# The order of 1230 tasks on five engines, replaced by another order

## The chip, the cores and the metric

The kernel runs on one core of a Trainium2 chip. The core has five engines with a queue each, which work their queues in order: TensorE (PE: matmuls into PSUM banks; PEld is its weight load), VectorE (DVE), ScalarE (ACT), GpSimd (POOL) and SyncE (SP, which here issues nearly all DMAs). Engines wait for each other by semaphores. The metric is the device time of one execution in microseconds (us).

## The reference, cut to what matters

One transformer block on 2048 tokens of width 512, all weights bfloat16. The modulation vectors come from a condition `c`; the attention is linear, with softmax features of 16 elements per head (32 heads), and a gated feed-forward part follows.

```python
mod = (_silu(c) @ w_mod).reshape(c.shape[0], 6, 1, -1)      # sa, ca, ga, sb, cb, gb
h = _layernorm(x) * (1 + ca) + sa
q, k, v = split_heads(h @ wqkv)
phi = lambda t: concat(softmax(t @ w_phi), softmax(-(t @ w_phi)))
kv, z = einsum(phi(k), v), sum(phi(k))                       # over all tokens
o = einsum(phi(q), kv) / (einsum(phi(q), z) + 1e-6)
x = x + ga * (o @ wo)
h = _layernorm(x) * (1 + cb) + sb
x = x + gb * ((sigmoid(h @ w_gate) * (h @ w_up)) @ w_down)
```

## The kernel before, in words

Tokens are cut into 16 tiles of 128. Everything is written as small tasks, each with its engine, what it reads and writes, and the buffers it uses. A string, `ORDER`, lists all 1230 tasks by name; `G.arrange` walks it, gives each task its engine (the default one, or the one behind an `@`: A is ACT, D is DVE, P is POOL), hands out buffer slots in that order, and the tasks are then emitted one by one. So the string alone sets what follows what in each engine's queue, and which earlier task must have let go of a buffer or of one of the eight PSUM banks.

```python
t.eng = LETTER[e] if e else next(iter(t.alts))
assert t.eng in t.alts and t.deps <= done and t not in done, name
for b in t.bufs:
    if b.slot is None:
        b.slot = slots[b.cls].pop(0)
```

The tasks by name, with their lines:
- `ld_...` are loads on SP (x in seven pieces, L537; the first two modulation blocks in four, L542; the key weights `wk`, L545, and value weights `wv`, L551; the attention gate's block `wmga`, L555; the rest of `w_mod`, `wmm2`, L556). `wqT0` to `wqT3` (L669) load the query weights by a DMA that transposes them.
- `warm...` (L600) are matmuls on zeros that nobody reads. `ld_wd2`, which writes the rows that they read, waits for all of them.
- `modc1.0` and `modc1.1` (L630) are the first modulation's products, in two halves of the width, 16 matmuls of one column each; `modc1c0`, `modc1c1` copy the sums.
- `tpw`, `wTc`, `fold1j`, `foldc1j` transpose the key weights on PE and multiply them by the feature weights (L661 to L685); `fold0j`, `foldc0j` do that for the query weights, `fold0j` reading what `wqTj` brought.
- `st1`, `rs1`, `nmr1`, `xn1` are the first layernorm; `tph` (L744) transposes a tile group on PE and `hm1` (L751, L753) modulates it. Layernorm groups are the tiles 0, 1, (2,3), (4,5) and so on; `hm1_23` is block 3 of group 2. Groups 6 and 7 are transposed by DMA (`xT1`, L736).
- `K`, `V`, `Q` (L817, L821, L871) are four matmuls of 512 columns for a tile, K in two halves for tiles 0 to 7 (`K0a` needs only blocks 0 and 1) and V for tiles 0 to 3. `e`, `n`, `r`, `phi` make the key features: exponentials on ACT (L776), sums on DVE (L780), reciprocals, products on DVE or POOL (L787); tiles 11 and 13 to 15 are cut in four or two parts. `qe`, `qn`, `qphi` and a DMA transpose `pT` do it for the queries. `va` copies V. `kv` (L282) adds up over tiles; `kvn`, `kvz` (L294, L299) read the sums out.
- Per tile then `num`, `rd`, `u` (attention out), `oT`, `out` (L356), `x1`, the second layernorm `st2` to `xn2`, `xnT`, `mod` (the second modulation), and per chunk of tiles (1, 1, 2, 4, 4, 4) the gated part: `g`, `u` (L447), `tg` (ACT), `hm` (DVE), `y` (L485), `fin`, and the store `st`.

`num0a` is the first task that needs the sum over all tokens; PE does `Q` of seven tiles ahead of it and of the others behind it.

Of the kernel before, what the change touches and what calls it, by code (L numbers as in the profile page):

```python
# [43 lines left out]
wqT1 hm1_22 hm1_13@A hm1_03 xn1_7 K1a K0a hm1_02@A hm1_23@A xn1_6 tph42 tph40 xn1_5 hm1_40@A st1_8 tph41 ld_x3a xn1_4 K3a hm1_42 hm1_12@A ld_wv0 nmr1_6 tph43
K3b hm1_41@A xn1_11 tph30 xn1_10 st1_9 rs1_5@P hm1_30@A tph31 wqT3 tph32 K1b ld_wmga st1_15 st1_14 hm1_31@A fold01 foldc01 K0b tph33 wqT2 rs1_8@P K2a K2b
hm1_33 nmr1_5 V0a wqT0 V0b V3a xn1_9 e3.0 V1a xT1_11 e0.0 fold03 n3.0 V1b nmr1_8 xn1_14 va0 e2.0 n0.0 st1_13 r0.0 modca.0 modca.1 xn1_15 st1_12 xn1_8 foldc03
n2.0 modcac e1.0 hm1_32@A V2a fold02 phi0.0 n1.0 r1.0 fold00 V2b foldc02 foldc00 r3.0 va1 xT1_10 hm1_60@P ld_wmm2 va2 r2.0@A hm1_62@P tph82 hm1_82@A tph50
phi2.0@D phi1.0@D hm1_50@A hm1_63@P V3b K4a K4b rs1_7@P Q0 Q2 kv0.0 Q1 qe0.0 va3 qe2.0 hm1_43@A qe1.0 modc2.0 tph52 modc2.1 tph51 nmr1_7 xn1_12 xn1_13
phi3.0@D ld_wo qn0.0 modc2c e4.0 kv1.0 qn2.0 hm1_52 kv2.0 Q4 K5a kv3.0 xT1_12 xT1_13 qphi0.0@P qphi0.1@P qn1.0 qe4.0 qphi2.1 tph80 K5b hm1_80@A hm1_51@A e5.0
pT0 qphi2.0 n4.0 r4.0@A qn4.0 n5.0 phi4.0@D qphi1.1@P hm1_61@P qphi1.0@P tph53 V5 K7a V4 va5 hm1_53@A V6 pT2 hm1_70@P qphi4.1 va4 hm1_71 mask4 va6 K6a K7b K6b  # L50
e6.0 K8 tph83 hm1_83 r5.0 qphi4.0@P e8.0 pT1 pT4 ld_wd2 tph81 hm1_81 n6.0 n8.0 e7.0 n7.0 V7 kv4.0 hm1_72@P K11 K9 V9 K14 V8 r6.0@A e9.0 va7 va9 r7.0@A e11.2
# [4 lines left out]
kv14.0 kv15.0 qn6.0 kvn0 kvz0 kv13.4 kv14.4 kv15.4 kvz1 kvn1 num0a num1a num2a wo2 rd0a wo_all rd1a qe3.0 u0a num0b num4a num1b rd0b Q11 qe5.0 rd2a u0b u2a
rd4a num2b qn3.0 u1a rd1b tpo0 Q8 qphi6.0@P qphi6.1@P oT0 out0 num4b rd2b u1b wd0 qe11.0 u2b qphi3.1@P qphi3.0@P x1_0 rd4b st2_0 qe8.0 Q7 qe7.0 tpo1 oT1 Q10
Q9 out1 Q15 oT2 rs2_0 qn5.0 nmr2_0 xn2_0 u4a u4b x1_1 qn7.0 tsw xnT0 out2 qphi5.1@P qphi5.0@P pT6 mod02 mod00 qphi7.0@P pT3 mod03@A mod01@A qe15.0 qphi7.1@P
Q13 g0.8 x1_2 tg0.8 g0.1 st2_1 wd1 rs2_1 tg0.1 u0.8 u0.1 g0.0 num3b g0.4 hm0.1 hm0.8 pT5 qe9.0 tg0.4 g0.9 wd2 u0.4 u0.9 rd3b u3b tg0.9 g0.5 num3a hm0.4 hm0.9
# [999 lines left out]
```

## Time and profile before

| what | us |
|---|---|
| three runs | 204.16, 204.36, 204.45 (median 204.36) |
| the profiled execution, first to last instruction (its span) | 202.6 |
| granted TensorE clock over the span | 1.000 |

The profiled execution's time is given by its span alone; its distance to the median of the runs is 1.8 us, which lies around the span. In the views below PE, PEld, DVE, ACT and POOL are the engines; "x16" is a count; in the timeline and the chain the first number is the start in us, the second the length; in brackets stands how long the engine sat idle before, and what ended that.

### The profile page before, as it was taken

How to read it: one execution, taken by the hardware profiler on the slowest of the kernel's cores; microseconds unless marked ns; L12 is line 12 of the kernel's file. 1: busy time of each engine (PE TensorE's matmuls, PEld its weight loads, DVE VectorE, ACT ScalarE, POOL GpSimd, SP SyncE). 2: the span in 40 equal slices, each digit the busy share in tenths (PEclk: the TensorE clock that was granted, in tenths of full speed). 3: DMA queues.
4: the chain of work that ended last, by engine and by line, in shares of the span. 5: the costliest groups of instructions: out<-in, count | busy, mean ns of one | idle time of the engine just before them, and what ended most of it. 6: DMA issues, size and time to landing. Idle time of an engine off the chain costs nothing.

```text
span 202.6 us, 4159 instructions
## 1 busy us (share of the span) xinstructions
PE 195.7 (97%) x1471; PEld 106.2 (52%) x1471; DVE 160.4 (79%) x375; ACT 106.1 (52%) x252; POOL 102.8 (51%) x144
## 2 busy tenths in 40 slices
PE   7889999999999999999999999999999999999993
PEld 2455565455464787668844444444444444444442
DVE  3899999999999999998897797884969754326622
ACT  3899999999978984566441215212113320334100
POOL 5598987888699998866670066230030332000000
PEclk9999999999999999999999999999999999999999
DMA  6999966559953962419645233542113031000011
GB/s 173 329 248 265 264 237 119 111 80 290 402 204 71 137 102 59 80 28 108 128 75 84 53 71 84 102 107 53 26 26 81 2 78 52 31 3 22 33 53 55
DMA packets 49452, 22.92 MB, mean 113 GB/s; under 512 B 38065, under 2 KB 47634, under 8 KB 49426
## 3 DMA queue, kind: packets, MB, share of 16 engines
q1 hardware_dynamic: 48896, 22.59, 48.9%
q8 instruction: 12, 0.20, 0.4%
q14 instruction: 14, 0.11, 0.2%
q10 hardware_dynamic: 530, 0.02, 0.1%
HBM read 11.58 MB, written 2.10 MB: 68 GB/s over the span
## 4 chain that ended last, share of the span: by engine, by line
PE 69%; DVE 14%; ACT 6%; issue 3%; POOL 3%; DMA 3%; SPq 1%; DVEq 0%; POOLq 0%
PE y_ps L485 19%; PE u_ps L447 18%; PE g_ps L447 17%; DVE ks L780 7%; PE a_ps L356 6%; DMA wqk_sb<-in_A_wqkv_dram 3%; PE num L326 2%; DVE kr L798 2%; ACT qe L776 2%; DVE phi L787 2%; PE q_ps L871 1%; PE g_ps L449 1%; ACT h1T L751 1%; DVE qks L780 1%; POOL phi L787 1%
## 5 line engine op out<-in xcount | busy, mean ns | idle before, releaser
L457 ACT ACTIVATE tg<-g_ps 128x512 bf16<-128x512 f32 (+5 forms) x66 | 28.8, 455 | 67.0 <-PE g_ps L447 39.4
L485 PE MATMUL y_ps<-wd_sb,wmod_sb 128*128 128x512 bf16 (+4 forms) x187 | 45.7, 367 | 0.0
L468 DVE SCALAR_TENSOR_TENSOR wmod_sb<-tg,u_ps 128x512 bf16<-128x512 bf16 (+4 forms) x63 | 30.2, 491 | 18.1 <-ACT tg L457 11.6
L447 PEld LDWEIGHTS <-wg_sb 128*128 128x128 bf16 (+1 forms) x252 | 21.9, 99 | 16.1
L447 PEld LDWEIGHTS <-wu_sb 128*128 128x128 bf16 (+1 forms) x252 | 21.9, 99 | 16.0 <-issue 0.3
L784 POOL TENSOR_TENSOR qphi<-qe,qks 128x512 bf16<-128x512 bf16 x24 | 25.1, 1062 | 4.4 <-DMA pT<-qphi 1.7
L485 PEld LDWEIGHTS <-wmod_sb 128*128 128x128 bf16 (+1 forms) x187 | 17.1, 98 | 16.0 <-issue 0.6
L447 PE MATMUL u_ps<-wT_sb,wu_sb 128*128 128x512 bf16 (+2 forms) x124 | 23.8, 322 | 0.0
L447 PE MATMUL g_ps<-wT_sb,wg_sb 128*128 128x512 bf16 (+2 forms) x124 | 23.2, 322 | 0.0
L447 PE MATMUL g_ps<-wqk_sb,wg_sb 128*128 128x128 bf16 (+4 forms) x128 | 20.0, 287 | 0.0
L447 PE MATMUL u_ps<-wqk_sb,wu_sb 128*128 128x128 bf16 (+4 forms) x128 | 19.8, 287 | 0.1
L780 DVE TENSOR_REDUCE qks<-qe 128x64 bf16<-128x1024 bf16 x16 | 19.2, 1206 | 0.0
L492 DVE TENSOR_TENSOR ot<-y_ps,x 128x512 bf16<-128x512 f32 (+2 forms) x17 | 11.1, 654 | 10.2 <-PE y_ps L485 10.1
L780 DVE TENSOR_REDUCE ks<-e 128x64 f32<-128x1024 bf16 (+2 forms) x22 | 19.1, 903 | 0.0
L376 POOL TENSOR_SCALAR ve<-mv 128x2 f32<-128x2 f32 (+1 forms) x8 | 1.8, 221 | 33.8 <-DVE mv L366 33.7
L776 ACT ACTIVATE e<-k_ps 128x512 bf16<-128x512 f32 (+2 forms) x44 | 18.2, 522 | 0.0
L776 ACT ACTIVATE qe<-q_ps 128x512 bf16<-128x512 f32 x32 | 17.4, 618 | 0.6 <-POOL phi L787 0.4
L817 PE MATMUL k_ps<-wqk_f,h1T 128*128 128x512 bf16 x64 | 16.5, 379 | 0.0
L356 PE MATMUL a_ps<-wo_sb,oT 128*128 128x512 bf16 x64 | 16.3, 379 | 0.0
L787 POOL TENSOR_TENSOR phi<-e,kr 128x1024 bf16<-128x1024 bf16 (+2 forms) x10 | 14.4, 1449 | 3.5 <-ACT kr L795 2.0
L821 PE MATMUL v_ps<-wv_sb,h1T 128*128 128x512 bf16 x64 | 16.1, 379 | 0.1
L871 PE MATMUL q_ps<-wqk_f,h1T 128*128 128x512 bf16 x64 | 15.9, 379 | 0.0
(132 smaller groups left out, 306.7 us busy)
## 6 DMA issues: line engine op xcount, KB each, us to landing
out_dram<-ot SPq DMA_DIRECT2D x15, 128.0 KB, 1.7
x_sb<-in_A_x_dram SPq DMA_DIRECT2D x6, 256.0 KB, 5.4
wmod_sb<-in_w_mod_dram SPq DMA_DIRECT2D x1, 1536.0 KB, 6.8
wu_sb<-in_B_w_up_dram SPq DMA_DIRECT2D x1, 1376.0 KB, 10.7
wg_sb<-in_B_w_gate_dram SPq DMA_DIRECT2D x1, 1376.0 KB, 10.6
wd_sb<-in_B_w_down_dram SPq DMA_DIRECT2D x1, 1280.0 KB, 7.7
wmod_sb<-in_w_mod_dram SPq DMA_DIRECT2D x4, 256.0 KB, 6.3
wqk_sb<-in_A_wqkv_dram SPq DMA_DIRECT2D x2, 256.0 KB, 4.8
```

The costliest lines, as they stand in the source:

```text
L356: pe.matmul(ap_[:], lhsT=oT[:, j, :], rhs=wo_sb[:, j, :], start=(j == 0), stop=(j == KT - 1))
L447: pe.matmul(ps[:fsz, 0:n], lhsT=w[:, j, ft * P:ft * P + fsz], rhs=h[:, j, 0:n], start=(j == 0), stop=(j == KT - 1))
L457: G.add(f"tg{k}.{ft}", {"ACT": 0.13 + n * 0.00083}, lambda e, tg=tg, g_ps=g_ps, fsz=fsz, n=n: act.activation(tg[:fsz, 0:n], g_ps[:fsz, 0:n ...
L468: dve.scalar_tensor_tensor(hm_all[:fsz, hm[k].slot, ft, 0:n], tg[:fsz, 0:n], 1.0, u_ps[:fsz, 0:n], op0=ALU.add, op1=ALU.mult)
L485: mm = pe.matmul(y[:, 0:c1 - c0], lhsT=hm_all[:fsz, hm[k].slot, ft, tl * P:(tl + 1) * P], rhs=wd_sb[:fsz, ft, c0:c1], start=(ft == 0), sto ...
L776: act.activation(ee[:, a:b, s].rearrange("p g f h -> p g (f h)"), kp[:, a * 64:b * 64].rearrange("p (g n) -> p g n", n=64), ACT.Exp, scale ...
L780: dve.tensor_reduce(ks[:, a:b].rearrange("p g s h -> p (g s) h"), ee[:, a:b].rearrange("p g s f h -> p (g s) h f"), axis=AX.X, op=ALU.add)
L784: engine(e).tensor_tensor(ph[:].rearrange("p (g s f h) -> p g s f h", s=2, f=DH, h=4)[:, :, s], ee[:, :, s], ks[:, :, 1 - s].unsqueeze(2). ...
L787: engine(e).tensor_tensor(ph[:, a * P:b * P].rearrange("p (g f h) -> p g f h", f=DH, h=4), ee[:, a:b].rearrange("p g s f h -> p (g s) f h" ...
L817: pe.matmul(kp[:], lhsT=h1T[:, j, t * P:(t + 1) * P], rhs=wqk_f[:, j, D:2 * D], start=(j == 0), stop=(j == KT - 1))
L821: pe.matmul(vp[:], lhsT=h1T[:, j, t * P:(t + 1) * P], rhs=wv_sb[:, j, :], start=(j == 0), stop=(j == KT - 1))
L871: pe.matmul(qp[:], lhsT=h1T[:, j, t * P:(t + 1) * P], rhs=wqk_f[:, j, 0:D], start=(j == 0), stop=(j == KT - 1))
```

## The change

The string `ORDER` is replaced by another; nothing else of the kernel changes (the new string has one line less, so lines behind it are numbered one lower). All tasks stay; their places change on all engines, and for some of them the engine. The first lines of the two:

```diff
-wdz pmem warm0 ld_x0a st1_1 rs1_1 st1_0 c1 c2 ld_x0b warm1_0 warm1_1 warm1_2 warm1_3 ld_wk0 ld_wk1 nmr1_1 xn1_1@A st1_3 warm1_4 st1_2 rs1_0 xn1_0 tph11 tpw1
...
+wdz pmem warm0 ld_x0a st1_0 c1 ld_x0b st1_2 warm1_0 warm1_1 st1_3 rs1_2 warm1_2 warm1_3 warm1_4 rs1_0@P xn1_0 warm1_5 warm1_6 warm1_7 ld_wk0 tpw0 wTc0 tpw1 wTc1
```

**SP's queue, the loads of the first 20 us.** `x_sb` is the input, `wmod_sb` the first modulation blocks, `wv_sb` the value weights, `wT_sb` the transposed query weights, and `wqk_sb<-in_w_mod_dram` the attention gate's block. Before:

```order
L542 DMA wmod_sb<-in_w_mod_dram 128x4x256 x2
L537 DMA x_sb<-in_A_x_dram 128x2x512
L542 DMA wmod_sb<-in_w_mod_dram 128x4x256 x2
L537 DMA x_sb<-in_A_x_dram 128x2x512
L669 DMA_TRANSPOSE wT_sb<-in_A_wqkv_dram 128x4x128
L537 DMA x_sb<-in_A_x_dram 128x4x512
L551 DMA wv_sb<-in_A_wqkv_dram 128x4x512
L669 DMA_TRANSPOSE wT_sb<-in_A_wqkv_dram 128x4x128
L555 DMA wqk_sb<-in_w_mod_dram 128x4x512
L669 DMA_TRANSPOSE wT_sb<-in_A_wqkv_dram 128x4x128 x2
```

The same place of the change:

```order
L541 DMA wmod_sb<-in_w_mod_dram 128x4x256 x2
L536 DMA x_sb<-in_A_x_dram 128x2x512
L541 DMA wmod_sb<-in_w_mod_dram 128x4x256 x2
L536 DMA x_sb<-in_A_x_dram 128x4x512
L536 DMA x_sb<-in_A_x_dram 128x2x512
L550 DMA wv_sb<-in_A_wqkv_dram 128x4x512
L668 DMA_TRANSPOSE wT_sb<-in_A_wqkv_dram 128x4x128
L554 DMA wqk_sb<-in_w_mod_dram 128x4x512
L668 DMA_TRANSPOSE wT_sb<-in_A_wqkv_dram 128x4x128 x3
L555 DMA wmod_sb<-in_w_mod_dram 128x4x1536
```

The transpose that stood ahead of the last x piece and the value weights now stands in the group of three behind the gate's block; the transposes come in the order 2, 0, 1, 3 (before 1, 3, 2, 0).

**PE's queue, around the second modulation half.** `tp_h` are the transposes of layernormed tiles, `k_ps` is a key product, `modc_ps` the modulation's sum, of which the first of 16 matmuls is shown. Before:

```order
L744 LDWEIGHTS xn
L744 MATMUL tp_h<-ident,xn 128x128
L744 LDWEIGHTS xn
L744 MATMUL tp_h<-ident,xn 128x128
L630 LDWEIGHTS wmod_sb
L630 MATMUL modc_ps<-sc_bf,wmod_sb 128x1
```

The change:

```order
L743 LDWEIGHTS xn
L743 MATMUL tp_h<-ident,xn 128x128
L816 LDWEIGHTS h1T
L816 MATMUL k_ps<-wqk_f,h1T 128x512
L816 LDWEIGHTS h1T
L816 MATMUL k_ps<-wqk_f,h1T 128x512
L743 LDWEIGHTS xn
L743 MATMUL tp_h<-ident,xn 128x128
L629 LDWEIGHTS wmod_sb
L629 MATMUL modc_ps<-sc_bf,wmod_sb 128x1
```

`K0a`, two matmuls, and a transpose now stand ahead of `modc1.1`; before, the first key product came behind it.

**ACT's queue, around the folded query weights.** `e<-k_ps` are the exponentials of key tiles, `vaug<-v_ps` copies of V, `wqk_f<-fold_ps` the copies `foldc0j`. Before:

```order
L685 CAST wqk_f<-fold_ps 128x512
L776 ACTIVATE e<-k_ps 128x8x64 x4
L836 CAST vaug_110<-v_ps 128x32x16
L776 ACTIVATE e<-k_ps 128x8x64 x2
L685 CAST wqk_f<-fold_ps 128x512
L648 COPY gcol<-modc_ps 128x4
L776 ACTIVATE e<-k_ps 128x8x64 x2
```

The change:

```order
L775 ACTIVATE e<-k_ps 128x8x64 x2
L835 CAST vaug_110<-v_ps 128x32x16
L750 ACTIVATE h1T<-tp_h,modc 128x256 x3
L835 CAST vaug_111<-v_ps 128x32x16
L684 CAST wqk_f<-fold_ps 128x512
L647 COPY gcol<-modc_ps 128x4
L684 CAST wqk_f<-fold_ps 128x512
L775 ACTIVATE e<-k_ps 128x8x64 x2
```

Before, a fold's copy stood ahead of the first exponentials and another in the midst of them; now two copies and the gate's copy stand between the second and the third key tile's exponentials. On PE `fold00` and `fold01` stand side by side ahead of `K1a`.

Other moves that the prediction speaks of: ahead of the key sums' end (`kvn0`) DVE has one whole, one half and three quarter-tile `phi` less, and POOL as much more; POOL takes the layernorm pieces `rs1_0` and `xn1_1` from ACT; one `warm` matmul moves from the start to the place just ahead of `num0a`; all four `mod0` of tile 0 are on ACT (before two on DVE); the load of `w_gate` moves ahead of the query features' transposes, those of `w_up` and `w_down` stay behind them.

More of the change, by code (lines that the diff above doesn't have):

```diff
@@ L44 @@
[L44 to L51, printed above, removed]
@@ L56 @@
[L56 to L59, printed above, removed]
@@ new lines @@
+ld_x1b st1_1 nmr1_2 tph00 c2 st1_7 warm1_8 warm1_9 tph03 bd fold10 foldc10 ld_wk1 fold11 tpw3 tpw2 rs1_1@P warm1_10 wTc3 c3 foldc11 fold13 wTc2 xn1_3 xn1_2
+st1_6 rs1_4@P foldc13 nmr1_1 ld_x1a st1_5 xn1_1 fold12 tph20 foldc12 st1_4 nmr1_4 ld_wm00b ld_wm00a rs1_3 modc1.0 tph01 modc1c0@D hm1_01@A xn1_6 xn1_7 ld_x2b
+tph10 tph12 hm1_20@A tph22 tph21 hm1_00 K0a st1_11 hm1_21@A ld_wm01a nmr1_3 xn1_5 xn1_4 st1_10 tph11 hm1_11@A hm1_10@A rs1_6@P ld_wm01b modc1.1 modc1c1@D hm1_03
+tph23 hm1_23@A K2a hm1_12@A tph02 hm1_02@A tph43 hm1_43@A K3a hm1_22 K2b e2.0 ld_x3a st1_13 st1_12 rs1_7@P nmr1_6 tph33 xn1_11 ld_x2a st1_8 tph40 K3b xn1_10
@@ new lines @@
+tph13 hm1_33@A K0b tph32 e0.0 hm1_40 st1_9 ld_wv0 rs1_5@P hm1_13 V3a nmr1_7 xn1_13 xn1_12 V3b tph31 va3 V0a hm1_31@A V0b V2a tph30 hm1_32@A wqT2 ld_wmga n0.0
+wqT0 mask4 wqT1 nmr1_5 st1_14 xn1_8 xn1_9 fold00 hm1_30@A r0.0 st1_15 va0 fold01 foldc01 K1a modca.0 modca.1 modcac K1b foldc00 rs1_8@P wqT3 fold03 e1.0 fold02
+foldc02 V1a tph41 V1b phi0.0 foldc03 hm1_41 V4 V2b e3.0 n2.0 r2.0@A n1.0 va1 va2 r1.0 phi1.0@D nmr1_8 tph51 tph53 hm1_53 hm1_51 Q0 qe0.0 qn0.0 Q4 tph42 hm1_42@A
+phi2.0 ld_wmm2 modc2.0 modc2.1 qe4.0 K6a tph52 kv0.0 kv1.0 va4 hm1_52@A modc2c Q2 qe2.0 n3.0 tph50 hm1_50@A kv2.0 qphi0.0 K4a r3.0 phi3.0@D K4b e4.0 K6b Q1
@@ new lines @@
+r11.6 phi11.6 e10.0 r11.4@A e12.0 n14.0 r14.0@A phi11.0 n10.0 r10.0@A n12.0 phi11.4 K13 kv8.0 kv9.0 phi14.0 va11 r14.4 phi14.4 phi10.0@D e13.4 n13.4 e13.0 n13.0
+gwa gra wo0 r13.0 phi13.0 e15.0 n15.0 r15.0 V10 V14 V12 Q6 V15 va10 kv10.0 kv11.4 kv11.0 kv11.6 kv11.2 r12.0@A phi12.0@D e15.4 V13 n15.4 r13.4 r15.4 Q5
+phi15.4@D va12 kv12.0 va14 qe6.0 qn6.0 Q3 va13 kv13.0 kv14.0 va15 phi15.0 kv15.0 kvz0 phi13.4 kv13.4 kv14.4 kv15.4 warm1_11 kvn0 num0a kvn1 kvz1 num1a wo2 wo1
+wo3 rd0a num2a u0a qphi6.1@P num0b rd0b u0b qphi6.0@P Q7 qe3.0 qe5.0 qn3.0 qphi3.0@P num1b rd1b rd1a u1b tpo0 oT0 ld_wu0 ld_wd qphi3.1@P rd2a wo_all qe7.0 Q11
@@ new lines @@
+qe11.0 num2b rd2b out0 u1a ld_wd2 grb wd1 x1_0 Q8 qe8.0 num4a Q10 tpo1 num4b st2_0 u2b u2a rd4b pT6 rs2_0 oT1 nmr2_0 xn2_0 tsw qn5.0 qphi5.1@P qphi5.0@P u4b oT2
+rd4a u4a Q9 Q13 qn7.0 xnT0 mod01@A pT3 mod02@A mod00@A mod03@A out1 x1_1 st2_1 Q15 qe15.0 out2 g0.1 qphi7.1@P tg0.1 g0.8 qphi7.0@P tg0.8 x1_2 u0.8 hm0.8 u0.1
+hm0.1 qe9.0 g0.9 num3b tg0.9 g0.4 tg0.4 rd3b u3b g0.5 u0.9 hm0.9 u0.4 hm0.4 num3a qe10.0 rs2_1 nmr2_1 u0.5 tg0.5 rd3a u3a u0.10 g0.10 tg0.10 g0.0 hm0.5 hm0.10
+g0.3 num6a tg0.0 rd6a pT5 u0.0 hm0.0 num5a u6a num6b u0.2 g0.7 g0.2 rd5a u5a rd6b u6b xn2_1 oT4 out4 tg0.2 hm0.2 tg0.7 qe13.0 x1_4 u0.6 u0.7 hm0.7 pT7 g0.6
@@ L87 @@
+y12.10 fin12 st12 y15.7 y15.8 y15.9 y15.10 fin15 st15 y15.0b y15.1b y15.2b y15.3b y15.4b y15.5b y15.6b y15.7b y15.8b y15.9b y15.10b fin15b st15b
 """
```

62 lines of the change are left out of this document (28 added, 34 removed).

## The prediction

> **What bounds the kernel now.** I read the page first: the span and how busy each engine is.
>
> ```profile
> span 202.6 us, 4159 instructions
> PE 195.7 (97%) x1471; PEld 106.2 (52%) x1471; DVE 160.4 (79%) x375; ACT 106.1 (52%) x252; POOL 102.8 (51%) x144
> PE 69%; DVE 14%; ACT 6%; issue 3%; POOL 3%; DMA 3%; SPq 1%; DVEq 0%; POOLq 0%
> ```
>
> PE is busy almost throughout, and the chain that ended last is mostly PE. The window view then cuts the span where the program changes character: at 13.22 PE begins the second modulation product, at 57.64 the first readout `num0a`.
>
> ```profile
> 13.22:57.64 44.42, 43.81 (x415) 24.48 (x416) 43.90 (x93) 43.44 (x118) 37.83 (x42) 1.00 0.88 230
> ...
> 100.00:199.23 99.23, 99.19 (x533) 46.32 (x529) 67.70 (x143) 24.84 (x44) 20.85 (x33) 1.00 0.25 55
> ```
>
> Columns: length, then PE, PEld, DVE, ACT and POOL busy. In the first stretch PE, DVE and ACT are all full and POOL has 6.6 us left. From 100 on only PE counts. "Busy" includes a matmul's drain, so I count work by start-to-start times from the chain:
>
> ```profile
> 56.99 0.37 DVE kvb L294
> 57.64 0.93 PE num L326 x24
> ...
> 75.46 0.45 PE u_ps L447 x8
> ...
> 99.88 0.26 PE num L326 x8
> ...
> 170.42 1.73 PE u_ps L447 x8
> ...
> 199.23 0.29 DVE ot L492
> ```
>
> So a matmul of 512 columns costs 0.216 us (1.73/8), one of 128 columns 0.056, one of 68 columns 0.0325. Between 13.22 and 57.64 PE issues 156 of 512 columns (64 K, 64 V, 28 Q: 33.7 us), 128 of 68 (kv: 4.2), 51 of 128 (16 fold, 35 transposes: 2.9) and 80 of one column. The last cost about 0.025 each: 16 of them took 0.55 us in the row at 13.22 below, of which about 0.17 is the drain of the last. That is 2.0. The sum is 42.8 in 44.42 us: PE has **1.6 us of slack** there, a part of it the wait for `kvb` (chain row at 56.99). Behind 57.64 the same PE tasks run in both kernels, and so do the last tile's products and `fin15b`, so the 3.4 us from 199.23 to the span's end stay.
>
> **The change part by part.** The start first, by PE's timeline:
>
> ```profile
> 1.25 2.74 PE L600 MATMUL warm<-wd_sb 128*128 128x512 bf16 x6 [1.25 <-DVE wd_sb L593]
> ...
> 10.76 0.55 PE L630 MATMUL modc_ps<-sc_bf,wmod_sb 128*128 128x1 bf16 x16
> ...
> 13.22 0.55 PE L630 MATMUL modc_ps<-sc_bf,wmod_sb 128*128 128x1 bf16 x16 [0.48 <-ACT h1T L751]
> ...
> 13.84 0.38 PE L817 MATMUL k_ps<-wqk_f,h1T 128*128 128x512 bf16 x1
> ```
>
> *Key products of tile 0 begun early.* `K0a` needs only the first modulation half, whose product runs at 10.76. Its sum ends at 11.3; a small copy and the two modulations of tile 0 on DVE and ACT (0.34 each, row of L753 below) follow, so it can start near 12.2. PE must still stop for the second half, whose loads keep their places in SP's queue, so `modc1.1` stays near 13.2. The move takes two matmuls out of the full stretch (0.43), one transpose enters it (0.06), and the warm matmul now placed just ahead of `num0a` enters too (0.22). Net **-0.16 us**.
>
> *Loads.* SP's queue is the part with a price. Its rows now:
>
> ```profile
> 8.40 0.84 SPq L537 DMA_DIRECT2D x_sb<-in_A_x_dram  x1
> 9.28 1.51 SPq L669 DMA_TRANSPOSE wT_sb<-in_A_wqkv_dram  x1
> 10.84 0.57 SPq L537 DMA_DIRECT2D x_sb<-in_A_x_dram  x1
> 11.46 0.50 SPq L551 DMA_DIRECT2D wv_sb<-in_A_wqkv_dram  x1
> 12.01 1.62 SPq L669 DMA_TRANSPOSE wT_sb<-in_A_wqkv_dram  x1
> 13.67 0.58 SPq L555 DMA_DIRECT2D wqk_sb<-in_w_mod_dram  x1
> 14.30 3.07 SPq L669 DMA_TRANSPOSE wT_sb<-in_A_wqkv_dram  x2
> ```
>
> And what the four weight transposes take from issue to landing (the view of their line), then where PE uses them (its timeline):
>
> ```profile
> L669 SPq DMA_TRANSPOSE wT_sb<-in_A_wqkv_dram x4: 1275/1564/1754, 9.3 to 16.1; - x4
> ...
> DMA to landing us min/median/max: 5.1/6.3/7.4
> ```
>
> ```profile
> 16.79 0.39 PE L679 MATMUL fold_ps<-bd,wT_sb 128*128 128x128 bf16 x4
> ...
> 18.42 1.89 PE L821 MATMUL v_ps<-wv_sb,h1T 128*128 128x512 bf16 x8
> 20.15 0.39 PE L679 MATMUL fold_ps<-bd,wT_sb 128*128 128x128 bf16 x4
> ...
> 21.86 0.61 PE L679 MATMUL fold_ps<-bd,wT_sb 128*128 128x128 bf16 x8
> ```
>
> Before, one transpose went out at 9.28, ahead of the value weights, and served the fold at 16.79; the other folds stood at 20.15 and 21.86, late enough for their data. Now all four go behind the value weights, and PE has `fold00` and `fold01` side by side ahead of `K1a`. PE would be ready for `fold01` at 13.22 + 0.4 (`modc1.1`) + 20 x 0.216 (five K and five V halves) + 20 x 0.056 (16 transposes, `fold00`) = 19.1. When does the third transpose, which `fold01` needs, land? Two ways. By issue: 8.40 + 0.84 + 0.57 + 0.50 + 1.6 + 0.58 + 1.6 and small gaps gives 14.3, and with the median of 6.3 it lands at 20.6 (with 5.1: 19.4; with 7.4: 21.7). By likeness: behind the value weights stands the same row as before, transpose, 512 KB, transpose, transpose, whose third served the fold at 21.86; it moves up by what left its front, one transpose and the near-idle stretch behind it:
>
> ```profile
> DMA  9999999120399999999999999999999990000099
> GB/s 303 305 315 329 288 264 94 38 34 17 107 378 217 340 373 336 336 348 365 336 344 365 340 262 373 356 279 319 352 328 328 281 241 20 20 25 18 18 223 283
> DMA packets 4213, 2.47 MB, mean 247 GB/s; under 512 B 2223, under 2 KB 4212, under 8 KB 4212
> ```
>
> (11 to 21 us, a slice is 0.25 us: five slices near idle from 12.5.) That is 1.25 to 1.65 us, hence 20.2 to 20.6. I take **20.4**: PE stands still for 1.3 us (bounds 0.3 and 2.6). Behind `fold01` on PE wait `K1a`, the attention gate's product, and everything else; on ACT the copy `foldc01` stands ahead of the next exponentials, so ACT idles with it.
>
> *Engines.* DVE's window up to `kvn0`, and the groups (by form) that move:
>
> ```profile
> 3.59:56.94 53.35, 52.06 (x117) 1.00 0.94 240
> ```
>
> ```profile
> L787 DVE TENSOR_TENSOR phi<-e,kr 128x1024 bf16<-128x1024 bf16 x7 | 4.7, 678 | 0.0
> ...
> L787 DVE TENSOR_TENSOR phi<-e,kr 128x256 bf16<-128x256 bf16 x3 | 0.8, 300 | 0.0
> L753 DVE TENSOR_SCALAR h1T<-tp_h,modc 128x128 bf16<-128x128 bf16 x2 | 0.7, 335 | 0.0
> ...
> L787 POOL TENSOR_TENSOR phi<-e,kr 128x1024 bf16<-128x1024 bf16 x5 | 9.6, 1914 | 1.1 <-ACT kr L795 0.8 <-DVE kr L798 0.2
> ```
>
> DVE gives away one whole, one half and three quarter feature products (about 1.6 us by these rows, less their overlap) and gets a modulation, a reciprocal and two small ones (0.7): about 0.9 less, so it could reach `kvn0` at 56.0 in place of 56.94. ACT loses about 2.4 us (a layernorm, two modulations). Both gains lie beside PE, which needs to 57.3 anyway, and part of them goes into the wait for `foldc01`; they count as nothing. POOL gets about 7 us (a whole product 1.9, a half 1.0, three quarters 1.7, a modulation 0.5, a layernorm 1.8), some 1.8 of them ahead of 13.22, which uses up its 6.6 us of idle time. Summed by these rows in the new order from 4.5 us on, its last feature product ends near 55; PE asks for it near 57: hidden, by 2 us. Without that cover each us late is a us on the end.
>
> *Sum, against the profiled span.* `num0a` at 13.22 + 42.8 - 0.16 + 1.3 + 0.2 (small waits, as the two or three of before) = 57.3, which is 0.3 ahead of 57.64. Behind it I add 0.1: before, PE hardly waits there, so a new order can only lose. Span 202.4. The span is 1.8 us under the median of the runs, 204.36, and that rest stays: **204.2 us**. In short: time = 204.36 + (landing of the third transpose - 20.6). A measurement here tells 0.2%, 0.41 us, from no change: faster needs a landing before 20.2, slower one after 21.0.
>
> **The rivals.**
> *Transposes in time.* If the near-idle stretches come from plain loads waiting behind a lone transpose, three in a row lose none of it. From 13.2 to that landing 2.2 MB move; at the 350 GB/s of the good slices this takes 6.3 us, landing 19.5, and the time is 203.3. For it speaks the steady 330 to 370; against it the mean of 247 over the ten us. The Trainium skill, page "DMA: Bandwidth & Descriptors", section "Where 436 GB/s comes from", has about 358 GB/s as what HBM gives one core; by that rule the landing would be an estimated 19.4 and the wait nearly gone, and the good slices agree with it while the mean of the same window doesn't.
>
> *Transposes late, slower.* At the mean rate of 247 GB/s the same 2.2 MB take 9 us: landing 22.2, PE idle 3.1 us, ACT's exponentials late by the same, and the time 206.0; with the slowest transpose of before (7.4) 205.5. It decides from a landing of 21.0. For it: three transposes and 512 KB share the queue. Against: the issue is 1.5 us earlier than before.
>
> *A wait in the readout.* All four modulations of tile 0 go to ACT:
>
> ```profile
> 67.10 0.81 ACT L426 ACTIVATE wqk_sb<-tp_x,modc 128x128 bf16<-128x128 bf16 x2
> ...
> 68.75 0.46 ACT L457 ACTIVATE tg<-g_ps 128x128 bf16<-128x128 f32 x2
> ```
>
> Two more are 0.8 us on ACT ahead of the first `tg`. The last bias load of `w_down` also waits for the warm matmul at 57, and the gate row that POOL's `wd1` needs is queued behind it. If PE's banks run out for that time it costs about 0.8: 205.0. Against: PE has 10 us of queries and outputs as filler between `num0a` and the first `g`.
>
> *The clock.* The six first matmuls stand 0.43 us apart, twice the later 0.216. Had PE a long hole behind its start, 3.4 us at half rate would cost 1.7 us: 205.9. The Trainium skill, "TensorE: Matmul & The Clock Gate", section "What's actually happening", says that an idle window of about 3.4 us halves the clock; by it a wait of 1.3 us does nothing, and the trace shows clock 1.00 behind 13.22 with no hole to try it on.
>
> **How the numbers follow.** Forecast 0.40 (204.2; mostly within 0.2%, 0.10 of it faster, 0.03 slower), transposes in time 0.28 (203.3), late 0.17 (205.5 to 206.0), readout 0.10 (205.0, 0.03 of it within), clock 0.05 (205.9). Faster 0.10 + 0.28 = 0.38, same 0.27 + 0.03 = 0.30, slower 0.32. The forecast's own range is 203.8 to 204.8. The range for all goes from 202.9 (landing before 19.1, nothing left to wait for) to 205.6, which leaves out the clock and the far end of the late case.
>
> **What would show it.** In the changed profile: two `k_ps` matmuls on PE ahead of the second `modc_ps`, near 12.2; that `modc_ps` still near 13.2; a hole on PE of 0.3 to 2.6 us just ahead of the folds at 19 to 21; DVE's `kvb` before 57 and `num0a` near 57.3; POOL's last `phi` before 57; the stretch behind `num0a` as long as before, 141.6 us to the last `ot`. A hole elsewhere on PE, above all from 60 to 100, or `kvb` ending later than PE is ready, would make the prediction wrong.

## The result, and the profile after

| | before | changed |
|---|---|---|
| runs shown with the change, us | 203.75 to 204.45, median 204.26 (4) | 210.95 to 212.69, median 211.21 (4) |
| span of the profiled execution | 202.6 | 208.9 |
| `num0a` begins | 57.64 | 63.47 |
| from there to the span's end | 144.96 | 145.43 |

The ratio is 1.036 (95% interval 1.0325 to 1.040): slower, and outside the range of the prediction, which had 204.2 and at most 205.6. Of the 6.3 us of span 5.8 are lost ahead of `num0a`, 0.5 behind it. The page of the changed kernel (span, busy time, chain of waits by engine):

```profile
span 208.9 us, 4150 instructions
PE 198.4 (95%) x1471; PEld 106.7 (51%) x1471; DVE 165.5 (79%) x374; ACT 105.5 (50%) x246; POOL 108.5 (52%) x150
PE 58%; DVE 10%; DMA 10%; POOL 7%; SPq 7%; ACT 4%; issue 3%; POOLq 0%; DVEq 0%
```

PE's share of the chain fell from 69% to 58%; something else now ends the waits. The window view of the changed kernel, for the stretch from the second modulation product to `num0a`, and for VectorE's from its first instruction to `kvn0` (length, then PE, PEld, DVE, ACT, POOL busy, clock, DMA share, GB/s):

```profile
13.28:63.47 50.19, 45.97 (x418) 24.63 (x416) 47.33 (x85) 44.85 (x116) 45.16 (x49) 0.98 0.76 196
...
3.71:62.91 59.20, 53.99 (x493) 29.19 (x492) 55.92 (x114) 50.83 (x131) 52.49 (x62) 0.97 0.82 219
```

PE, 43.81 busy of 44.42 before, is now 45.97 of 50.19: it waits. VectorE is busy for 55.92 us ahead of `kvn0`, 3.9 more than the 52.06 of before, though by the rows of before it was given 0.9 less to do. The groups of VectorE in that stretch, by form, show where. The changed kernel:

```profile
L786 DVE TENSOR_TENSOR phi<-e,kr 128x1024 bf16<-128x1024 bf16 x6 | 7.1, 1178 | 0.1
L786 DVE TENSOR_TENSOR phi<-e,kr 128x512 bf16<-128x512 bf16 x1 | 1.1, 1093 | 0.1
```

and the halves before:

```profile
L787 DVE TENSOR_TENSOR phi<-e,kr 128x512 bf16<-128x512 bf16 x2 | 0.7, 388 | 0.0
```

A whole key product took a mean of 1.18 us; before it was 0.678 (the row of seven in the prediction). The half took 1.09, where the two of before take 0.388 on average. That is 8.2 us for work that 6 x 0.678 + 0.39 = 4.5 should do: **3.7 us more, with the same shapes on the same engine**. VectorE's timeline and POOL's beside it, at the worst of them:

```profile
27.54 1.90 DVE L786 TENSOR_TENSOR phi<-e,kr 128x1024 bf16<-128x1024 bf16 x1
```

```profile
26.97 1.92 POOL L786 TENSOR_TENSOR phi<-e,kr 128x1024 bf16<-128x1024 bf16 x1 [1.11 <-ACT kr L794]
```

POOL's product ends at 28.89. VectorE's begins 1.35 us ahead of that moment, while POOL's is running, and ends 0.55 behind it. It looks as if it had stood still until POOL was done. The other long ones (at 33.59, 41.21, 48.42, 58.49, 60.69) also begin while a POOL instruction runs. The rest of the start and the end of the stretch, from PE's timeline (start, length; idle before in brackets):

```profile
12.36 1.01 PE L816 MATMUL k_ps<-wqk_f,h1T 128*128 128x512 bf16 x2 [0.17 <-ACT h1T L750]
13.17 0.31 PE L743 MATMUL tp_h<-ident,xn 128*128 128x128 bf16 x1
13.28 0.61 PE L629 MATMUL modc_ps<-sc_bf,wmod_sb 128*128 128x1 bf16 x16
...
20.21 0.40 PE L678 MATMUL fold_ps<-bd,wT_sb 128*128 128x128 bf16 x4 [0.19 <-DMA wT_sb<-in_A_wqkv_dram]
21.44 0.40 PE L678 MATMUL fold_ps<-bd,wT_sb 128*128 128x128 bf16 x4 [0.83 <-DMA wT_sb<-in_A_wqkv_dram]
...
63.47 0.68 PE L325 MATMUL num<-kvb,pT 128*128 128x68 bf16 x16 [0.93 <-DVE kvb L293]
```

`K0a` and `modc1.1` stand where the prediction put them, the wait for the transposes too, and at the end PE stands 0.93 us for VectorE's `kvb`. Behind the folds VectorE idles once:

```profile
24.25 0.41 DVE L752 TENSOR_SCALAR h1T<-tp_h,modc 128x256 bf16<-128x256 bf16 x1 [1.61 <-PE tp_h L743]
```

And the clock, by windows:

```profile
8.00:12.00 4.00, 2.71 (x46) 2.07 (x46) 3.75 (x17) 3.68 (x9) 3.92 (x7) 1.00 1.17 307
12.00:16.00 4.00, 3.83 (x33) 2.07 (x31) 3.86 (x13) 3.65 (x9) 3.57 (x6) 0.57 1.14 322
```

From 12 to 16 us TensorE was granted 0.57. So there were three suspects: VectorE's products beside POOL's (3.7 us), the wait for the transposes (1.0 on PE, 1.6 on VectorE) and the clock. One of the four runs had a mean clock of 1.000 and the same span, 208.9, which already spoke against the third.

### The profile page after: what moved, and what is told of

Its sections match the earlier page's. It is cut to its first block, busy times and chain, and to the rows that moved or that the text cites. A ratio compares the mean times of both kernels' runs of the same rounds, so it can differ in the third digit from the quotient of the medians.

```text
span 208.9 us, 4150 instructions
## 1 busy us (share of the span) xinstructions
PE 198.4 (95%) x1471; PEld 106.7 (51%) x1471; DVE 165.5 (79%) x374; ACT 105.5 (50%) x246; POOL 108.5 (52%) x150
## 4 chain that ended last, share of the span: by engine, by line
PE 58%; DVE 10%; DMA 10%; POOL 7%; SPq 7%; ACT 4%; issue 3%; POOLq 0%; DVEq 0%
PE y_ps L484 18%; PE u_ps L446 16%; PE g_ps L446 16%; DMA wd_sb<-in_B_w_down_dram 5%; PE a_ps L355 4%; POOL qphi L783 3%; DMA wT_sb<-in_A_wqkv_dram 3%; SPq L668 2%; SPq L536 2%; DMA gdr<-gcol 2%; POOL phi L786 2%; DVE qks L779 1%; SPq L541 1%; DVE phi L786 1%; PE num L325 1%
## 5 line engine op out<-in xcount | busy, mean ns | idle before, releaser
L456 ACT ACTIVATE tg<-g_ps 128x512 bf16<-128x512 f32 (+3 forms) x66 | 28.8, 458 | 72.8 <-PE g_ps L446 51.2
L484 PE MATMUL y_ps<-wd_sb,wmod_sb 128*128 128x512 bf16 (+4 forms) x187 | 44.8, 367 | 0.0
L783 POOL TENSOR_TENSOR qphi<-qe,qks 128x512 bf16<-128x512 bf16 x22 | 23.2, 1073 | 3.1 <-DVE qks L779 2.6
L786 POOL TENSOR_TENSOR phi<-e,kr 128x1024 bf16<-128x1024 bf16 (+2 forms) x15 | 20.1, 1352 | 1.8 <-ACT kr L794 1.4
L446 PE MATMUL g_ps<-wqk_sb,wg_sb 128*128 128x128 bf16 (+4 forms) x128 | 19.5, 287 | 0.0
L446 PE MATMUL u_ps<-wqk_sb,wu_sb 128*128 128x128 bf16 (+4 forms) x128 | 19.0, 287 | 0.1
L816 PE MATMUL k_ps<-wqk_f,h1T 128*128 128x512 bf16 x64 | 17.4, 396 | 0.2 <-ACT h1T L750 0.2
```

The lines of the kernel that those rows point to most:

```text
L446: pe.matmul(ps[:fsz, 0:n], lhsT=w[:, j, ft * P:ft * P + fsz], rhs=h[:, j, 0:n], start=(j == 0), stop=(j == KT - 1))
L456: G.add(f"tg{k}.{ft}", {"ACT": 0.13 + n * 0.00083}, lambda e, tg=tg, g_ps=g_ps, fsz=fsz, n=n: act.activation(tg[:fsz, 0:n], g_ps[:fsz, 0:n ...
L484: mm = pe.matmul(y[:, 0:c1 - c0], lhsT=hm_all[:fsz, hm[k].slot, ft, tl * P:(tl + 1) * P], rhs=wd_sb[:fsz, ft, c0:c1], start=(ft == 0), sto ...
L783: engine(e).tensor_tensor(ph[:].rearrange("p (g s f h) -> p g s f h", s=2, f=DH, h=4)[:, :, s], ee[:, :, s], ks[:, :, 1 - s].unsqueeze(2). ...
L786: engine(e).tensor_tensor(ph[:, a * P:b * P].rearrange("p (g f h) -> p g f h", f=DH, h=4), ee[:, a:b].rearrange("p g s f h -> p (g s) f h" ...
L816: pe.matmul(kp[:], lhsT=h1T[:, j, t * P:(t + 1) * P], rhs=wqk_f[:, j, D:2 * D], start=(j == 0), stop=(j == KT - 1))
```

## The experiments

### Products by themselves

A kernel with VectorE's and GpSimd's instructions of this kind alone, in groups that begin together (`meet`). Two of its groups:

```diff
+    meet()
+    for _ in range(5):
+        prod(pool, ph_p)
+    for _ in range(8):
+        prod(dve, ph_d)
+    meet()
+    for _ in range(10):
+        prod(pool, ph_p, 0, 2)
+    for _ in range(8):
+        prod(dve, ph_d)
...
```

> A kernel of its own: only VectorE's and GpSimd's products, sums and fills in groups, the rest of the block left out (the output is a copy of x). Groups, in this order: 4 whole feature products on VectorE alone; 3 on GpSimd alone; 8 on VectorE beside 5 on GpSimd; 8 on VectorE beside 10 quarter products on GpSimd; 6 sums (one SBUF input) on VectorE beside 5 products on GpSimd; 6 products on VectorE beside 8 of GpSimd's layernorm steps (one input); 6 on VectorE beside 6 fills on GpSimd; 8 layernorm steps on VectorE beside 4 products on GpSimd. Theory 'one at a time' (a VectorE product of two SBUF inputs and a GpSimd instruction exclude each other, the one that began first keeps the other out until its end): alone 0.65 and 1.91 us; beside GpSimd's whole products the VectorE products that begin behind one take up to 1.9 + 0.6, those beside quarter products at most 0.6 + 0.6; sums stay at 1.20. Theory 'shared bandwidth': all VectorE products beside GpSimd's grow alike, to 0.9 or so, whatever the length of GpSimd's instruction. Theory 'no link' (the long products in the changed kernel came from waits on data that the trace counts as work): 0.65 and 1.91 everywhere.

Its timeline on VectorE, group by group (start, length, count; the second row shows the first five of eight products, those beside POOL's):

```profile
3.08 2.86 DVE L65 TENSOR_TENSOR ph_d<-ee,kr 128x1024 bf16<-128x1024 bf16 x4
...
13.27 11.45 DVE L65 TENSOR_TENSOR ph_d<-ee,kr 128x1024 bf16<-128x1024 bf16 x5
...
27.76 8.04 DVE L65 TENSOR_TENSOR ph_d<-ee,kr 128x1024 bf16<-128x1024 bf16 x8
...
37.95 7.48 DVE L69 TENSOR_REDUCE ks<-ee 128x64 f32<-128x1024 bf16 x6
...
48.53 6.94 DVE L65 TENSOR_TENSOR ph_d<-ee,kr 128x1024 bf16<-128x1024 bf16 x6
...
57.95 4.31 DVE L65 TENSOR_TENSOR ph_d<-ee,kr 128x1024 bf16<-128x1024 bf16 x6
...
64.64 9.55 DVE L72 TENSOR_SCALAR ph_d<-ee,rs 128x512 bf16<-128x512 bf16 x8
```

and POOL's, alone and beside VectorE's second group:

```profile
6.40 5.89 POOL L65 TENSOR_TENSOR ph_p<-ee,kr 128x1024 bf16<-128x1024 bf16 x3 [3.55 <-DVE ph_p L85]
...
13.00 11.17 POOL L65 TENSOR_TENSOR ph_p<-ee,kr 128x1024 bf16<-128x1024 bf16 x5
```

Alone a product takes 2.86/4 = 0.72 us on VectorE and 5.89/3 = 1.96 on POOL. Side by side the five of each take 11.45/5 = 2.29 and 11.17/5 = 2.23: the two engines take turns, one product each, and of the 2.68 us that a pair would take one behind the other only 0.4 is saved. Beside quarter products VectorE's take 8.04/8 = 1.0, beside one-input layernorm steps 6.94/6 = 1.16. In all three groups a product of VectorE ends 0.53 to 0.55 us behind the end of the POOL instruction that it met, so the wait grows with that instruction's length and isn't a share. Sums beside POOL's products take 7.48/6 = 1.25 (in the kernel before a mean of 1.20), and products beside POOL's fills (4.31/6 = 0.72) are as alone. The last row is a surprise: VectorE's one-input layernorm steps, whose last four (alone) took 0.41 each, took 1.79 to 1.95 beside POOL's products. "One at a time" held, the other two theories fell. The Trainium skill, page "Advanced Engine Details and Errata", section "Mode Summary", says that the second VectorE port to SBUF is shared with GpSimd and that the two block each other in 2-port instructions; "GPSIMD Engine Reference", section "1. Specifications", adds instructions with two SBUF inputs. The runs agree with both, as far as they show it (which mode the layernorm step ran in they don't), and give the size: VectorE waits for the end of the other engine's instruction.

### In place: the meetings taken away

The seven key products of VectorE ahead of `num0a` become sums over half a tile, with one SBUF input; `kv` of these tiles reads what they write.

```diff
             def f_p(e, s=0, a=a, b=b):
+                if (q, t, a) in ONE:
+                    fl = ee[:, a:b].rearrange("p g s f h -> p (g s f h)")[:, 0:(b - a) * 64]
+                    with nc.allow_low_precision(reason="as the sums of the queries"):
+                        dve.tensor_reduce(ph[:, a * P:a * P + P], fl.rearrange("p (o r) -> p o r", o=P), axis=AX.X, op=ALU.add)
+                    return
```

> The changed kernel with the seven key products that VectorE has ahead of the readout replaced by sums over half the tile (one SBUF input, about the same 0.65 us, the key sums of these tiles are then not the reference's); everything else, GpSimd's work too, is as in the changed kernel. Theory 'one at a time': these seven took 3.9 us more than 0.65 (0.37 for the half) each, and VectorE has hardly any idle time left there, so they end near their time alone, num0a comes at 59.5 to 61 in place of 63.3, and the run takes 207.5 to 209.0. Theory 'GpSimd has too much': its last feature product still ends at 61.5; 210.7 to 211.5. Theory 'the start' (held by the transposes and the slower clock between 10 and 23 us): 210.5 to 211.5.

> The kernel before with the nine whole and half key products of VectorE replaced in the same way (key sums not the reference's). Theory 'one at a time': in the order of before these products took 0.63 to 0.70 us, they hardly met GpSimd's; 203.7 to 204.5. If the replacement itself made work shorter (and not the meeting), the time would fall here as much as in the changed kernel: 201 to 202.5.

In the changed kernel: 207.14 us (206.60 to 209.03), 4.1 less; ratio to the kernel before 1.017 (1.011 to 1.022). In the kernel before: 204.03, ratio 1.000 (0.998 to 1.002). The replaced instructions took what they should, and `num0a` moved (changed kernel with the replacement: VectorE's group, PE's and POOL's timelines):

```profile
L787 DVE TENSOR_REDUCE phi<-e 128x128 bf16<-128x512 bf16 x6 | 3.8, 634 | 0.0
```

```profile
59.48 0.68 PE L327 MATMUL num<-kvb,pT 128*128 128x68 bf16 x16
```

```profile
57.22 1.05 POOL L793 TENSOR_TENSOR phi<-e,kr 128x512 bf16<-128x512 bf16 x1 [0.18 <-DVE kr L804]
```

In the change itself POOL's last three feature products were these:

```profile
57.92 3.58 POOL L786 TENSOR_TENSOR phi<-e,kr 128x512 bf16<-128x512 bf16 x3
```

`num0a` begins 4.0 us earlier, and POOL's last feature product ends at 58.27 in place of 61.50, though POOL's work is the same to the instruction. The order of before loses nothing that the replacement gives back, the changed order 4.1 us.

Does POOL's load do it, or the port? In the kernel before POOL stands idle for 1.0 us from 50.25 and for 1.3 us from 54.35 (brackets of the rows), just where VectorE makes its products:

```profile
51.28 3.07 POOL L787 TENSOR_TENSOR phi<-e,kr 128x512 bf16<-128x512 bf16 x3 [1.03 <-DVE phi L787]
55.61 1.16 POOL L787 TENSOR_TENSOR phi<-e,kr 128x512 bf16<-128x512 bf16 x1 [1.27 <-ACT kr L795]
```

Two more instructions on POOL, which nobody reads, were put there:

```diff
-phi14.4 phi14.0 kv10.0
+dum0 phi14.4 phi14.0 kv10.0
...
-qe6.0 va12 kv11.2 n15.0 r15.0 r15.4@A va13 phi13.4 Q5
+qe6.0 va12 kv11.2 n15.0 r15.0 r15.4@A va13 phi13.4 dum1 Q5
...
+    scr = cst.tile([P, 1024], BF16, name="scr")
+    for i in range(2):
+        G.add(f"dum{i}", {"POOL": 1.0}, lambda e: pool.tensor_tensor(scr[:, 0:512], bd[:].rearrange("p k m -> p (k m)"), bd[:].rearrange("p k m -> p (k m)"), op=ALU.mult), r=["bd"])
```

and in a second kernel `pool.memset(scr[:], 0.0)` in their place.

> The kernel before with two more products of two inputs on GpSimd, on data that nobody reads, 1.05 us each by its rows of 512 columns, put where GpSimd stands idle but VectorE makes its feature products: ahead of phi14.4 (idle 50.25 to 51.28) and behind phi13.4 (idle 54.35 to 55.61). Theory 'one at a time': VectorE's products at 50.1 to 51.4 and 54.6 to 55.9 wait for them, up to about 1 us each time, and kvn0 and the end come 0.6 to 1.8 later: 204.8 to 206.0. Theory 'GpSimd has too much' : the idle time takes them, at most 0.1 to 0.2 late: 204.1 to 204.4.

> The same with a fill of 0.95 us (no SBUF input) in place of each of the two products: GpSimd's time is taken as much, the port is not. Theory 'one at a time': 204.1 to 204.4, VectorE's products keep 0.3 to 0.7 us. If GpSimd's load is what counts, as e10.

With the two products 209.07 us (207.51 to 210.37), ratio 1.022 (1.017 to 1.027); with the two fills 204.25, ratio 1.003 (0.9997 to 1.006), which isn't told from none. VectorE's timeline with the products:

```profile
51.70 2.21 DVE L790 TENSOR_TENSOR phi<-e,kr 128x256 bf16<-128x256 bf16 x4
...
57.08 3.81 DVE L790 TENSOR_TENSOR phi<-e,kr 128x512 bf16<-128x512 bf16 x3
```

and with the fills:

```profile
50.05 1.36 DVE L790 TENSOR_TENSOR phi<-e,kr 128x256 bf16<-128x256 bf16 x4
...
54.57 1.29 DVE L790 TENSOR_TENSOR phi<-e,kr 128x512 bf16<-128x512 bf16 x3
```

The same seven products took 6.02 against 2.65 us: 3.4 more. The expectation (0.6 to 1.8) was too small because it counted the two new instructions alone. POOL's timeline shows what it missed:

```profile
56.81 1.04 POOL L591 TENSOR_TENSOR scr<-bd 128x512 bf16<-128x512 bf16 x1
57.91 1.13 POOL L790 TENSOR_TENSOR phi<-e,kr 128x512 bf16<-128x512 bf16 x1
59.00 4.04 POOL L854 TENSOR_TENSOR wo_sb<-wo_sb,ga_sb 128x512 bf16<-128x512 bf16 x3
```

Once POOL's idle time is gone its next real instructions follow without a gap, and VectorE's second and third product wait for these too. Part of the median of 209.07 is the clock's. Only the run of 207.51, 3.4 above before, kept it (mean 0.998); the other five had 0.992 or less. In the profiled one (210.37, mean 0.983) the clock fell between 14 and 18 us, and VectorE's first whole product, far ahead of both new instructions, came at 28.48 in place of 26.92. So about 3.4 us is the price of the two products; why the clock fell so early in most of these runs is not shown.

### The engines put back

The nine names alone, taken out of the lists:

```diff
-phi2.0 qphi2.1@P phi11.2 phi11.0 phi11.4 phi13.0 phi15.0 qphi0.0 phi15.4@D
+phi2.0@D qphi2.1 phi11.2@D phi11.0@D phi11.4@D phi13.0@D phi15.0@D qphi0.0@P phi15.4
```

> The changed kernel in its own order, with the nine feature products that changed engines ahead of num0a put back on the engine of before (seven to VectorE, two to GpSimd): VectorE has 1.5 us more to do by the times alone, GpSimd some 5 less. Theory 'VectorE's work alone': kvn0 1.5 later, 212 to 213. Theory 'one at a time': fewer of GpSimd's instructions stand in the way; what that gives back depends on where they fall, between 209 and 211.2.

214.05 us (212.84 to 215.07), ratio 1.048 (1.042 to 1.054): slower still, by more than either theory said. VectorE's products in it:

```profile
L787 DVE TENSOR_TENSOR phi<-e,kr 128x1024 bf16<-128x1024 bf16 x7 | 6.3, 907 | 0.1
L787 DVE TENSOR_TENSOR phi<-e,kr 128x512 bf16<-128x512 bf16 x2 | 2.6, 1325 | 0.3 <-DMA wd_sb<-in_B_w_down_dram 0.3
```

The whole ones meet POOL less (0.91 in place of 1.18), the two halves all the more (1.33 against 0.39 alone). So the sharing out of before doesn't mend this order; with the two runs above this points to when the products run.

### The wait for the transposes, and the clock

The folds moved back in the lists of PE and ACT, so that PE does `K1` first:

```diff
-xn1_9 fold00 hm1_30@A r0.0 st1_15 va0 fold01 foldc01 K1a modca.0 modca.1 modcac K1b foldc00 rs1_8@P wqT3 fold03
+xn1_9 hm1_30@A r0.0 st1_15 va0 K1a modca.0 modca.1 modcac K1b rs1_8@P wqT3 fold00 foldc00 fold01 foldc01 fold03
```

> The changed kernel with the first two folds of the query weights and their copies moved behind the attention gate's product and K1, to where the other two are, so that TensorE need not stand for the transposed weights. Theory 'the start': the hole of 1.0 us on TensorE ahead of 21.44 goes, and with it VectorE's idle 1.6 us at 22.6; 209.6 to 210.2 if that idle time is on the path. Theory 'one at a time' alone: VectorE is late through its products; what it gains here it loses again where its products meet GpSimd's; 210.5 to 211.3.

> The changed kernel with both: VectorE's seven key products replaced by sums over half the tile (key sums not the reference's), and the first two folds moved behind K1. If meeting at the memory port and the wait for the transposes are separate costs on one chain, they add: 211.2 - 4.1 - 0.8 = 206.3. If the wait was hidden behind the products, or the other way round, it is 207.1 again. What then is left over 204.2 is neither of the two.

Alone: 210.39 (210.03 to 211.68), ratio 1.033 (1.029 to 1.036), 0.8 less than the change, though the intervals overlap, and between the two forecasts. `num0a` moved by 0.7:

```profile
62.76 0.67 PE L326 MATMUL num<-kvb,pT 128*128 128x68 bf16 x16 [0.93 <-DVE kvb L294]
```

With the products replaced as well: 206.76 (206.18 to 207.30), ratio 1.012 (1.008 to 1.015). This is 0.4 below the replacement alone, `num0a` 0.3 earlier, at 59.16. In this order, with its clock as it is, the wait costs under a microsecond.

For the clock seven more `warm` matmuls on zeros were put between 9 and 12.5 us, into the list of the change and into the one with folds and products mended: one ahead of `fold13`, two ahead of `fold12`, one ahead of `tph20`, two ahead of `tph01`, one ahead of `K0a`; all are numbered anew.

```diff
-    for i in range(12):
+    for i in range(19):
         warm(f"warm1_{i}", 1, 0.22, r=["c1"], w=["warm"])
```

> The changed kernel with seven more matmuls on zeros between 9 and 12.5 us, where TensorE now stands for short times, so that its clock should stay at 1.00 (it was granted 0.54 and 0.61 from 12 to 16 us). If VectorE's chain ends the stretch to num0a, TensorE being slower ahead of it costs little: 210.8 to 211.3. If the clock's loss (key products 0.43 apart in place of 0.216, some 1.4 us) is on the path: 209.6 to 210.2.

> The changed kernel with VectorE's seven key products replaced (key sums not the reference's), the first two folds moved behind K1, and the seven more matmuls on zeros that keep TensorE's clock. If the clock is the next cost on the path: 205.3 to 205.9 (up to 1.4 less than 206.8). If VectorE, without an idle stretch of its own by then, still ends the part to num0a: 206.5 to 207.3.

The clock stayed up (the changed kernel with the seven):

```profile
8.00:12.00 4.00, 3.60 (x47) 2.10 (x46) 3.79 (x16) 3.13 (x7) 3.82 (x7) 1.00 1.17 308
12.00:16.00 4.00, 3.41 (x36) 2.04 (x38) 3.82 (x15) 3.69 (x11) 3.80 (x7) 1.00 1.21 307
```

and the time gained nothing: 212.10 us (211.47 to 212.74), ratio 1.039 (1.034 to 1.044), `num0a` at 63.14; with the other two mended 207.61 (207.35 to 207.89), ratio 1.016 (1.013 to 1.019), `num0a` at 59.17 as without. Both are slower than expected, by 0.8 and 0.3 us, and end later than their likes without the seven. Behind `num0a` each has one wait of PE that its like hasn't, for a transposed query tile, about as long as what it loses there; the row of the first, and the other has 1.15 at 93.25:

```profile
97.21 0.64 PE L326 MATMUL num<-kvb,pT 128*128 128x68 bf16 x8 [1.12 <-DMA pT<-qphi]
```

Why that DMA lands later there wasn't followed up. For `num0a` of this order keeping the clock up gave 0.3 us at most.

### The named part alone, and the two halves of the order

In the kernel before, `K0a` ahead of `modc1.1`, with what it needs (two small layernorm tasks, `st1_11` and `nmr1_4`, move behind that):

```diff
-rs1_4@P nmr1_4 ld_wm01a modc1c0 hm1_11@A hm1_10@A tph02 rs1_3@P tph01 tph23 hm1_20@A hm1_01@A st1_10 tph21 hm1_21@A hm1_00 modc1.1
+rs1_4@P ld_wm01a modc1c0 tph01 hm1_01@A hm1_00 st1_11 nmr1_4 hm1_11@A hm1_10@A tph02 rs1_3@P tph23 hm1_20@A st1_10 K0a tph21 hm1_21@A modc1.1
```

> The kernel before with nothing but the named part of the change: K0a ahead of modc1.1 on TensorE, with what it needs (hm1_00 and hm1_01) moved ahead on VectorE and ScalarE. By the prediction's term it takes two matmuls out of the full stretch, 0.1 to 0.4 us: 203.8 to 204.1. Rival: VectorE ends that stretch, and work moved on TensorE alone gives nothing: 204.1 to 204.3; or a bank is missed and modc1.1 comes later: 204.4 to 204.8.

205.05 us (204.36 to 206.40), ratio 1.003 (1.001 to 1.006): a little slower. PE's timeline:

```profile
13.18 0.27 PE L744 MATMUL tp_h<-ident,xn 128*128 128x128 bf16 x2 [0.55 <-ACT h1T L751]
13.29 0.59 PE L817 MATMUL k_ps<-wqk_f,h1T 128*128 128x512 bf16 x2
13.72 0.28 PE L744 MATMUL tp_h<-ident,xn 128*128 128x128 bf16 x2
13.88 0.54 PE L630 MATMUL modc_ps<-sc_bf,wmod_sb 128*128 128x1 bf16 x16
```

PE waits 0.55 us for ACT's modulation to let go of a bank all the same, and only then comes to `K0a`; `modc1.1` is at 13.88 in place of 13.22, and `num0a` at 58.50. The rival with the missed bank held in kind, though its 204.4 to 204.8 was passed.

Then the order was cut at `num0a`: the front of before with the rest of the change, and the reverse.

> The order of before as far as num0a, and behind it all other tasks in the order of the change. All theories that put the loss ahead of num0a (the port, the transposes, the clock): num0a at 57.6 as before, and the time 204.2 to 205.2, of which up to 1.0 is what the new order loses behind num0a. If the loss sat behind num0a: 208 or more.

> The reverse: the order of the change as far as num0a, and behind it the tasks in the order of before. Loss ahead of num0a: num0a at 63 again, 210.0 to 211.2. Loss behind it: 205 to 207.

Front of before: 204.76 us, ratio 1.003 (1.001 to 1.005), `num0a` at 57.34; the new rest costs 0.6 us here, with two small waits for DMA transposes that the kernel before hasn't (0.24 and 0.41 us at 72 to 74). Front of the change: `num0a` at 63.82, as late as in the change, but 216.99 us, ratio 1.062 (1.057 to 1.067), which the expectation missed by 6. PE's timeline there:

```profile
74.36 1.04 PE L356 MATMUL a_ps<-wo_sb,oT 128*128 128x512 bf16 x4 [1.78 <-DMA oT<-o]
...
80.42 0.30 PE L326 MATMUL num<-kvb,pT 128*128 128x68 bf16 x4 [3.05 <-DMA pT<-qphi]
```

The rest of before counts on queries that its own front had made ready; behind another front it waits for them. So this half says where the loss begins, and nothing of what the rest is worth.

## Why the prediction was wrong

The step that failed is the one on the **engines**. It let "both gains lie beside PE", took VectorE to reach `kvn0` at 56.0 with 0.9 us less to do, and POOL's last feature product to end near 55, "hidden, by 2 us". VectorE reached it at 62.91, POOL's product ended at 61.50. The durations were taken from rows of before and added up for each engine by itself. But on these two engines an instruction's length isn't its own: in the order of before VectorE's whole products began where POOL stood idle, was nearly through or was itself held up, and took 0.678. The trace of before hinted at it, in POOL's rows and VectorE's beside the second of them:

```profile
12.24 0.70 POOL L713 TENSOR_TENSOR rs<-ve,mhalf 128x2 f32<-128x2 f32 x1
...
26.95 1.15 POOL L713 TENSOR_TENSOR rs<-ve,mhalf 128x2 f32<-128x2 f32 x1
```

```profile
26.92 1.22 DVE L787 TENSOR_TENSOR phi<-e,kr 128x1024 bf16<-128x1024 bf16 x2
```

The same two-column instruction took 0.70 us and, beside VectorE's two products, 1.15. A mean by group hides that; single rows of one form, compared, show it.

Point by point:

- *PE bounds the stretch, with 1.6 us of slack.* So it was before. The prediction's own row, 52.06 busy of 53.35, showed VectorE with only 1.3 us left, less than PE has, and the argument didn't use it. VectorE got 3.7 us in products and 1.6 of idle time. With the products replaced and the folds moved `num0a` still came at 59.16, and with PE's clock kept up as well at 59.17: PE at full speed didn't bring it forward; it then stood for its loads (end of this section).
- *`K0a` early, -0.16 us.* The places were right (12.36 and 13.28). The gain lies in PE's time, which is not what ends the stretch, and done alone it lost 0.3% to a wait for a bank.
- *Loads.* Right in kind and near in size: 0.83 + 0.19 = 1.0 us of waiting against 1.3 forecast. The third transpose served PE at 21.44 in place of 20.4, within the bounds; that PE was ready for it at 20.6 and not at 19.1 is about half the clock's doing. From `modc1.1` until it was ready for the first fold PE took 6.74 us, and 5.96 in the run with seven more matmuls, which kept its clock. By the formula this alone would have been 204.36 + 21.4 - 20.6 = 205.2. Taking the wait away gave 0.8 of some 7 us.
- *The readout.* 0.5 us behind `num0a`, forecast 0.1. PE has no wait over 0.15 us from there to 190 us, so the four modulations on ACT held it up nowhere; where the 0.5 arises wasn't followed up.
- *The clock rival.* It came true as an event (0.57 granted from 12 to 16) but in this order not as a price: keeping the clock up gave 0.3 us at most. In the order of before it is a price, and about the 1.7 that the prediction gave it: of the twelve runs with the two fills the four with a mean clock of 0.992 took 205.64 to 206.06 us, the others, all at 0.996 or more, 203.75 to 204.82. The condition was wrong as well, see below.
- *What none of the rivals had*: a price that arises when two engines that share no data work at the same time.

The 5.8 us ahead of `num0a` are so made up: 4.0 from the products (shown by the replacement), 0.3 more when the folds move as well (0.7 when they move alone), and 1.5 that stays with both mended (`num0a` at 59.16 against 57.64). In the trace of that kernel stand, beside a start that is 0.16 later, 0.58 us more in the first layernorm step on VectorE, 0.26 in the three query products, and 0.78 in two waits of VectorE. Not all of that is what holds `num0a`: in the kernel with the clock kept up as well that step took 0.38 again and one of the two waits was gone, and `num0a` stayed. PE's rows there, and VectorE's:

```profile
20.02 0.69 PE L617 MATMUL modc_ps<-sc_bf,wqk_sb 128*128 128x1 bf16 x16 [0.39 <-DMA wqk_sb<-in_w_mod_dram]
...
21.94 1.10 PE L680 MATMUL fold_ps<-bd,wT_sb 128*128 128x128 bf16 x12 [0.55 <-DMA wT_sb<-in_A_wqkv_dram]
```

```profile
23.62 0.41 DVE L754 TENSOR_SCALAR h1T<-tp_h,modc 128x256 bf16<-128x256 bf16 x1 [1.19 <-PE tp_h L745]
```

PE comes earlier and stands for the gate's block and for a transposed weight, VectorE idles 1.19 us for PE, and from there it is busy for 34.01 of the 34.99 us up to `kvn0`. So the price of the clock and that of the loads aren't told apart by these runs, and what the 1.5 us is made of stays open.

## What to carry to other kernels

Before work is moved between or along VectorE and GpSimd, lay their timelines side by side: a product of VectorE with two SBUF inputs and a product or layernorm step of GpSimd take turns (2.29 us for a pair of products that take 0.72 and 1.96 alone), and VectorE's, when it comes second, ends only behind GpSimd's. A replay of measured task times doesn't see this, since it takes each time as the task's own; it needs a rule that lets only one of the two run at a time (sums and fills excepted). Idle time of GpSimd is then not free to fill: 2.1 us of products put into it cost VectorE 3.4.
